# First x tile of a gated S5/GELU kernel: its first slab by a DMA transpose on SyncE, its second by a plain load on ScalarE's queue

## The chip, the core and the metric

The kernel runs on one core of one Trainium2 chip. The metric is the device time of one execution in microseconds (us), taken as the median of several runs. Beside it there is one profiled execution, whose trace and profile page are read below.

## What is computed

x is 2048 tokens by 640 channels in bf16. Two branches read it and a gate for each token mixes them:

```python
g = sigmoid((x * gate_w).sum(-1, keepdims=True))
# branch a: a diagonal state-space model (S5)
Lam_bar = exp(exp(log_dt) * Lam);  B_bar = ((Lam_bar - 1) / Lam)[:, None] * B      # complex
Bu = x @ B_bar.T
h[t] = Lam_bar * h[t-1] + Bu[t]                                                  # over 2048 steps
a = 2 * real(h @ C.T) + x * Dskip
# branch b: a dense layer with GELU, F = 1728
b = gelu(x @ w1 + b1) @ w2 + b2
out = g * a + (1 - g) * b
```

## The kernel before

The tokens are worked on in four tiles (q = 0 to 3) of 512. TensorE needs x with channels on partitions, so each tile has a transposed copy `xT[q]`, which has five slabs of 128 channels x 512 tokens (k = 0 to 4). A second copy with tokens on partitions, `xn`, feeds the gate on VectorE. The weights `w1`, `B`, `w2` and `C` are loaded once and stay in SBUF.

TensorE's order is: a warm-up on constants (`warm`, L416), the first part of the GELU layer for tile 0 (`m1_first`, L653), the rest of that layer for tile 0 (`m1`, L675), the projection with B (`bproj`, L718), and then, tile by tile, the second dense layer (L1015, L809), the projection with C (L1085, L922), B and `m1` again. VectorE builds tables from Lambda and runs the scan. ScalarE evicts PSUM and applies GELU.

Every piece of work is an `op(...)` with an engine, an assumed duration, an assumed latency `lat`, the names that it reads and writes, and a priority. `Sched.order` (L43) simulates the engines with those assumed times and puts the operations of each engine in an order; this order is fixed when the kernel is built. So an engine waits at run time for whatever its next instruction needs, even where a later instruction could run. SyncE (SP) and ScalarE (ACT) also issue DMAs, each on its own queue; an issue takes its place in the order of its engine.

What the start of the kernel looks like:

- SP issues two loads of x (`xna0`, `xna1`: 256 tokens each, the first 256 channels, 128 KB each), then the w1 slabs 1 and 2, a DMA transpose for slab 2 of `xT[0]`, w1 slab 3, a DMA transpose for slabs 3 and 4, w1 slab 4, the rest of w1, and then DMA transposes of B and of the other x tiles.
- ACT issues w1 slab 0 after GpSimd's clearing of `rows` (L386), and then six small loads of vectors into `rows`.
- Slabs 0 and 1 of `xT[0]` are made on TensorE: eight 128x128 transposes through PSUM (`xt0` to `xt3`, L428, each two transposes) and four VectorE copies (`xc0` to `xc3`, L434). The first half of the tokens goes first, a filler matmul (`fill`, L441) stands behind it, and the first six output blocks of slab 0 are computed in halves of 256 tokens.
- `m1_first` computes eight output blocks of 128 features in eight PSUM banks, one slab at a time: for each slab k the blocks jf = 0 to 7. Two of these matmuls, (k 0, jf 7) and (k 1, jf 7), are put back behind slab 2's first seven, because bank 7 is used by the transposes and by `cols`.
- `cols` (L455) is one TensorE transpose of `rows`. VectorE copies its result (L460), and from there a chain of small ScalarE and VectorE steps, with two loads of ScalarE's tables, leads to the first GELU eviction (L662). `m1`'s first matmul (L675) writes bank 0, which that eviction frees.

Of the kernel before, what the change touches and what calls it, by code (L numbers as in the profile page):

```python
# [9 lines left out]
BF16 = mybir.dt.bfloat16  # L10
# [174 lines left out]
def bass_gated_mix__ssm_conv_s5__dense_activation_gelu__prompt_kernel(  # L185
# [40 lines left out]
    with ExitStack() as es:  # L226
# [83 lines left out]
        def inc(eng, ins):  # L310
            return E.inc(eng, ins, eng + "_s")

        def dma_inc(eng, ins, sem):
            SEM(sem)
            E.count.setdefault(sem, 0)
            ins.then_inc(sems[sem], 16)
            E.count[sem] += 16
            return (sem, E.count[sem])
# [7 lines left out]
        def d_mm(n):  # L326
            return n / 2400.0 + 0.004
# [7 lines left out]

        def load_T(name, sem, pairs, writes, prio, dur, lat=3.0, reads=()):
            def fn():
                t = None
                for dst, src in pairs:
                    t = dma_inc("sp", nc.sync.dma_start_transpose(dst, src), sem)  # L340
                return t
            return op(name, "sp", dur, reads, writes, fn, prio=prio, lat=lat)

# [8 lines left out]

        def xtrans(q, ks, prio, dur):
            load_T(f"xT{q}_{ks[0]}", f"l_xT{q}_{ks[0]}", [(xT[q][:, ks[0]:ks[-1] + 1, :], x2[q * 512:(q + 1) * 512, ks[0] * 128:(ks[-1] + 1) * 128])],
                   [("xT", q, k) for k in ks], prio, dur)

# [9 lines left out]

        KN = 2

        for h in range(2):
            load(f"xna{h}", "sp", f"l_xna{h}", xn[0][:, 2 * h:2 * h + 2, 0:KN * 128],  # L370
                 x2[h * 256:(h + 1) * 256, 0:KN * 128].rearrange("(c p) d -> p c d", p=128), [("xna", h)], 0.2 * h, dur=0.45, lat=2.0 + 0.4 * h)
        w1load(1, "sp", 1)
# [15 lines left out]
        op("rz", "pool", 0.2, (), list(ROWS) + [("b1b", 0), ("b1b", 1), "rz"], f_rz, prio=-90)  # L388
        w1load(0, "act", -110, reads=["rz"])
        for i, (nm, (r0, src)) in enumerate(ROWS.items()):  # L390
# [22 lines left out]
        def f_warm():  # L413
            t = None
            for n in (512,) * 5 + (384,):
                t = nc.tensor.matmul(PS[4][:, 0:n], one.broadcast_to([128, 128]), one.broadcast_to([128, n]), start=True, stop=True)  # L416
            return inc("pe", t)

        op("warm", "pe", 2.7, (), [("bank", 4)], f_warm, prio=-1000)

        for i, (k, c0, c1) in enumerate(((0, 0, 2), (1, 0, 2), (0, 2, 4), (1, 2, 4))):
            bank = (7, 6, 7, 6)[i]
            pt = PS[bank][:, :].bitcast(BF16)[:, 0:(c1 - c0) * 128]

            def f_xt(k=k, pt=pt, c0=c0, c1=c1):
                t = None
                for c in range(c0, c1):
                    t = nc.tensor.transpose(pt[:, (c - c0) * 128:(c - c0 + 1) * 128], xn[0][:, c, k * 128:(k + 1) * 128], ident[:, :])  # L428
                return inc("pe", t)

            op(f"xt{i}", "pe", 0.11 * (c1 - c0), [("xna", c0 // 2), "ident"], [("bank", bank)], f_xt, prio=-990 + i if i < 2 else 3.1 + 0.1 * i)

            def f_xc(k=k, pt=pt, c0=c0, c1=c1):
                return inc("dve", nc.vector.tensor_copy(out=xT[0][:, k, c0 * 128:c1 * 128], in_=pt))  # L434

            op(f"xc{i}", "dve", 0.42, [("bank", bank)], [("xT", 0, k, c0)], f_xc, prio=-2000 + i)

        def f_fill():
            t = None
            for _ in range(1):  # L440
                t = nc.tensor.matmul(PS[3][:, 0:256], one.broadcast_to([128, 128]), one.broadcast_to([128, 256]), start=True, stop=True)  # L441
            return inc("pe", t)

        op("fill", "pe", 0.11, [("xna", 0), "ident"], [("bank", 3)], f_fill, prio=-900)

        XK0 = [[("xT", 0, k)] for k in range(KD)]
        XK0[0] = [("xT", 0, 0, 0), ("xT", 0, 0, 2)]
        XK0[1] = [("xT", 0, 1, 0), ("xT", 0, 1, 2)]
        XT = {q: [("xT", q, k) for k in range(KD)] for q in range(1, NQ)}
        XT[0] = [t for x in XK0 for t in x]  # L450

# [4 lines left out]

        op("cols", "pe", 0.3, list(ROWS) + [("b1b", 0), ("b1b", 1), "ident"], [("bank", 7)], f_cols, prio=20.5)

# [130 lines left out]
        for ci, src in enumerate((A_B_re, A_B_im)):  # L589
            for i, (p0, p1) in enumerate(((0, 512), (512, KP * 128))):  # L590
                load_T(f"B{ci}{i}", f"l_B{ci}{i}", [(BT[:, ci, :, p0:p1], src[p0:p1, :])], [("BT", ci, i)], prio=30 + ci + 0.1 * i, dur=0.8 * (p1 - p0) / 128)
        xtrans(1, range(KD), 32, 3.4)
        load("gwb", "sp", "l_gwb", gwb[:, :], gate_w.partition_broadcast(128), ["gwb"], prio=32.2)
        load("xnb", "sp", "l_xnb", xn[0][:, :, KN * 128:D], x2[0:512, KN * 128:D].rearrange("(c p) d -> p c d", p=128),
             [("xn", 0, 0), ("xn", 0, 1)], 32.4, dur=1.0, lat=6.0, reads=[("xna", 0), ("xna", 1)])
        big = load("w2a", "sp", "l_w2a", W2sb[:, 0:NF - 1, :], B_w2[0:nmain, :].rearrange("(j p) d -> p j d", p=128), ["w2a"], prio=33, lat=8.0)
# [46 lines left out]
        def m1_first():  # L643
            late = [(0, NW - 1), (1, NW - 1)]
            seq = [(k, jf) for k in range(KD) for jf in range(NW) if (k, jf) not in late]
            i = seq.index((2, NW - 1))
            seq[i:i] = late
            steps = [(0, jf, h) for h in range(2) for jf in range(6)] + [(k, jf, None) for k, jf in seq if k or jf > 5]
            for k, jf, h in steps:
                t0, t1 = (0, 512) if h is None else (256 * h, 256 * h + 256)  # L650

                def f_mm(jf=jf, k=k, t0=t0, t1=t1):
                    return inc("pe", nc.tensor.matmul(PS[jf][:, t0:t1], W1sb[:, k, jf * 128:(jf + 1) * 128], xT[0][:, k, t0:t1],  # L653
                                                      start=(k == 0 and t0 == 0), stop=(k == KD - 1), skip_group_check=jf < 6))

                op(f"m1_0_{jf}_{k}_{t0}", "pe", d_mm(t1 - t0), (XK0[k] if h is None else XK0[k][h:h + 1]) + [w1tok(k, jf)], [("bank", jf)],
                   f_mm, prio=pe_prio())
            for jf in range(NW):
                ctr["bank"] += 1

                def f_ge(jf=jf):
                    return inc("act", nc.scalar.activation(Gl[0][:, jf, :], PS[jf][:, :], ACT.Gelu_apprx_tanh, bias=b1col[:, jf:jf + 1]))  # L662

                op(f"ge_0_{jf}", "act", d_act(512), [("bank", jf), "b1col"], [("gl", 0, jf)], f_ge, prio=10)
# [344 lines left out]
        def outsT(q, mid=None):  # L1009
# [58 lines left out]
            for d in range(KD):  # L1068

                def f_dx(d=d):  # L1070
                    for _ in range(14 if q == NQ - 2 else 0):
                        nc.scalar.nop(nofuse=True)
                    return inc("act", nc.scalar.activation(xT[q][:, d, :], xT[q][:, d, :], ACT.Copy, scale=cols2[:, 1, d:d + 1]))  # L1073

                op(f"dx_{q}_{d}", "act", d_act(512), [("cols2", 1)], XK0[d] if q == 0 else [("xT", q, d)], f_dx, prio=20)

# [125 lines left out]
```

## Time and profile before

| | |
|---|---|
| device time, median of 3 runs | 212.66 us (212.58 to 212.69) |
| device time of the profiled execution | 211.84 us |
| span of its trace, first to last instruction | 210.5 us |
| TensorE matmul busy | 206.9 us (98%) |
| VectorE / ScalarE busy | 191.0 us (91%) / 102.7 us (49%) |
| mean granted clock in the record | 1.000 |

The trace's span starts with the first instruction and ends with the last; 1.34 us of the profiled execution's own time lie around it. The profiled execution is 0.82 us shorter than the median of the runs, so differences are worked out within the trace and put on the median. A line such as `4.55 0.39 PE L428 MATMUL ... x4` of the timeline reads: start, time from the first start to the last end, engine, line of the kernel, operation, tiles, and how many instructions are merged. PE is TensorE's matmul side, PEld its weight loads; SPq and ACTq are the DMA issues of SyncE and ScalarE. A matmul's record is longer than the distance to the next one, because they are pipelined.

### The profile page before, as it was taken

The numbers are of one execution on the slowest core, as the hardware profiler recorded it, in microseconds if no ns is written. First come the engines' busy times: TensorE is split into PE (matmuls) and PEld (weight loads), VectorE is DVE, ScalarE is ACT, GpSimd is POOL, SyncE is SP. The second block draws the span as 40 slices with busy tenths as digits, with TensorE's granted clock in tenths as the row PEclk, the third lists the DMA queues.
The fourth block names the chain that finished last, engine by engine and source line by source line (L and its number), as shares of the span: only waits on it lengthen the run. The fifth ranks groups of instructions, "written<-read, shape, count | busy, mean of one in ns | idle before, by whom it ended". The sixth has DMA issues, their size and how long they took to land.

```text
span 210.5 us, 2557 instructions
## 1 busy us (share of the span) xinstructions
PE 206.9 (98%) x987; PEld 95.1 (45%) x1004; DVE 191.0 (91%) x244; ACT 102.7 (49%) x166; POOL 4.2 (2%) x12
## 2 busy tenths in 40 slices
PE   8999999999999999999999999999999999999996
PEld 4544444444444444444444444444444444444444
DVE  2499999999999999999999999899999999899482
ACT  2398556679850533556683222455664253204321
POOL 1000000030000000000000000000010000000000
DMA  6999999999500020053373000006631000006623
GB/s 191 271 230 124 200 204 226 361 190 207 129 0 4 0 50 0 0 107 65 80 61 113 3 0 0 0 2 140 142 87 58 0 0 4 0 2 145 135 71 100
DMA packets 50248, 19.47 MB, mean 93 GB/s; under 512 B 43068, under 2 KB 48828, under 8 KB 50236
## 3 DMA queue, kind: packets, MB, share of 16 engines
q1 hardware_dynamic: 47904, 17.59, 38.2%
q0 software_dynamic: 1600, 1.32, 4.3%
q10 hardware_dynamic: 732, 0.40, 0.7%
q8 instruction: 8, 0.13, 0.3%
q14 instruction: 4, 0.03, 0.1%
HBM read 8.68 MB, written 2.63 MB: 54 GB/s over the span
## 4 chain that ended last, share of the span: by engine, by line
PE 98%; issue 0%; DVE 0%
PE ps L675 22%; PE ps L718 20%; PE ps L1015 20%; PE ps L1085 15%; PE ps L809 5%; PE ps L653 4%; PE ps L922 4%; PE ps L829 1%; PE ps L416 1%; PE ps L696 1%; PE ps L882 1%; PE ps L1050 1%; PE ps L428 0%; PE ps L846 0%; DVE W1sb L954 0%
## 5 line engine op out<-in xcount | busy, mean ns | idle before, releaser
L675 PE MATMUL ps<-xT,W1sb 128*128 128x512 bf16 x214 | 47.5, 379 | 0.3
L762 DVE TENSOR_TENSOR_SCAN W<-atab,V 128x1280 bf16<-128x1280 f32 x16 | 44.3, 2812 | 0.3
L718 PE MATMUL ps<-xT,BT 128*128 128x512 bf16 x196 | 43.3, 379 | 0.2
L1015 PE MATMUL ps<-Gl,W2sb 128*128 128x512 bf16 x192 | 42.8, 379 | 0.2
L682 ACT ACTIVATE Gl<-ps,cols 128x512 bf16<-128x512 f32 x44 | 29.8, 695 | 15.5 <-PE ps L675 15.5
L675 PEld LDWEIGHTS ps<-xT,W1sb 128*128 128x128 bf16 x220 | 21.5, 98 | 26.0
L1085 PE MATMUL ps<-Hb,CT 128*128 128x512 bf16 x150 | 32.9, 379 | 0.0
L729 ACT ACTIVATE U<-ps 128x512 bf16<-128x512 f32 x40 | 23.7, 596 | 15.5 <-PE ps L718 15.5
L718 PEld LDWEIGHTS ps<-xT,BT 128*128 128x128 bf16 x200 | 19.4, 98 | 23.8 <-ACT Gt L704 0.4
L1015 PEld LDWEIGHTS ps<-Gl,W2sb 128*128 128x128 bf16 x195 | 18.9, 98 | 23.3 <-issue 0.7
L1023 ACT ACTIVATE E1T<-ps,cols 128x512 bf16<-128x512 f32 x15 | 10.0, 686 | 26.2 <-PE ps L1015 14.7
L1085 PEld LDWEIGHTS ps<-Hb,CT 128*128 128x128 bf16 x150 | 14.7, 98 | 17.7
L1093 ACT ACTIVATE E2T<-ps 128x512 bf16<-128x512 f32 x15 | 9.0, 597 | 21.7 <-PE ps L1085 21.7
L627 DVE SCALAR_TENSOR_TENSOR trf<-xn,gwb 128x640 bf16<-128x640 bf16 x16 | 13.2, 823 | 0.4
L505 DVE TENSOR_TENSOR V<-V,W 128x1280 bf16<-128x1280 bf16 x16 | 12.5, 821 | 0.3
L505 DVE TENSOR_TENSOR Hb<-Hb,V 128x1280 bf16<-128x1280 bf16 x16 | 12.5, 821 | 0.3
L505 DVE TENSOR_TENSOR V<-mr,U 128x2560 bf16<-128x2560 bf16 x8 | 11.9, 1492 | 0.3
L505 DVE TENSOR_TENSOR Hb<-c,W 128x2560 bf16<-128x2560 bf16 x8 | 11.9, 1490 | 0.2
L809 PE MATMUL ps<-W2sb,Gl 128*128 128x512 bf16 x51 | 11.8, 379 | 0.1
L505 DVE TENSOR_TENSOR V<-s,W 128x2560 bf16<-128x2560 bf16 x8 | 11.9, 1484 | 0.0
L505 DVE TENSOR_TENSOR W<-mi,U 128x2560 bf16<-128x2560 bf16 x8 | 11.9, 1483 | 0.0
L1073 ACT ACTIVATE xT<-xT,cols 128x512 bf16<-128x512 bf16 x15 | 10.0, 712 | 0.0
(103 smaller groups left out, 148.2 us busy)
## 6 DMA issues: line engine op xcount, KB each, us to landing
W2sb<-in_B_w_dram SPq DMA_DIRECT2D x1, 2080.0 KB, 8.4
out_dram<-xn SPq DMA_DIRECT2D x3, 640.0 KB, 5.5
xn<-in_A_x_dram POOLq DMA_DIRECT2D x2, 640.0 KB, 7.0
W1sb<-in_B_w_dram SPq DMA_DIRECT2D x4, 256.0 KB, 4.0
trf<-grow SPq DMA_DIRECT2D x4, 256.0 KB, 4.9
xn<-in_A_x_dram SPq DMA_DIRECT2D x1, 640.0 KB, 7.2
W1sb<-in_B_w_dram SPq DMA_DIRECT2D x1, 480.0 KB, 5.6
W1sb<-in_B_w_dram SPq DMA_DIRECT2D x1, 400.0 KB, 6.4
```

The lines of the kernel that those rows point to most:

```text
L505: return inc("dve", nc.vector.tensor_tensor(out=o, in0=a, in1=b, op=o_))
L627: t = inc("dve", nc.vector.scalar_tensor_tensor(out=scr[:, :], in0=xn[q % 2][:, c, :], scalar=1.0, in1=gwb[:, :], op0=ALU.mult, op1=ALU.mu ...
L675: t = nc.tensor.matmul(PS[bank][:, :], W1sb[:, k, jf * 128:(jf + 1) * 128], xT[q][:, k, :], start=(k == 0), stop=(k == KD - 1))
L682: return inc("act", nc.scalar.activation(Gl[q % 2][:, jf, :], PS[bank][:, :], ACT.Gelu_apprx_tanh, bias=b1col[:, jf:jf + 1]))
L718: t = nc.tensor.matmul(PS[bank][:, :], BT[:, ci, kd, k * 128:(k + 1) * 128], xT[q][:, kd, :], start=(kd == 0), stop=(kd == KD - 1))
L729: return inc("act", nc.scalar.activation(dst, src, ACT.Copy, scale=1.0 if ci == 0 else -1.0))
L762: t = inc("dve", nc.vector.tensor_tensor_scan(out=g[:, ci, :], data0=a, data1=v[:, ci, :], initial=0.0, op0=ALU.mult, op1=ALU.add))
L809: t = nc.tensor.matmul(PS[bank][:, :], Gl[q % 2][:, jf, t4 * 128:(t4 + 1) * 128], W2sb[:, jf, 0:DN], start=False, stop=False, skip_group_c ...
L1015: t = nc.tensor.matmul(PS[bank][:, :], W2sb[:, jf, d * 128:(d + 1) * 128], Gl[q % 2][:, jf, :], start=(jf == 0 and not lead), stop=(jf == ...
L1023: return inc("act", nc.scalar.activation(E1T[:, d, :], PS[bank][:, :], ACT.Identity, bias=cols2[:, 0, d:d + 1]))
L1073: return inc("act", nc.scalar.activation(xT[q][:, d, :], xT[q][:, d, :], ACT.Copy, scale=cols2[:, 1, d:d + 1]))
L1085: t = nc.tensor.matmul(PS[bank][:, :].rearrange("p (s t) -> p s t", s=2), CT[:, ci, k, d * 128:(d + 1) * 128], Hb[:, 2 * (q % 2):2 * (q % ...
```

## The change

Slab 0 of `xT[0]` is loaded by one DMA transpose of 512 tokens x 128 channels, which is SP's first instruction. Slab 1 is loaded with tokens on partitions, by one plain load of 512 rows of 256 bytes (128 KB), which ACT issues behind w1 slab 0; four TensorE transposes and one VectorE copy of 512 columns make it. The w1 slab 0 load no longer waits for the clearing of `rows`. The warm-up gets one more matmul of 512 columns, the filler goes, slab 0's matmuls are whole (512 tokens), and `cols` comes earlier in `m1_first`. The later load of the rest of `xn` becomes two loads, since channels 0 to 127 have not been loaded in that layout.

```diff
-        for h in range(2):
-            load(f"xna{h}", "sp", f"l_xna{h}", xn[0][:, 2 * h:2 * h + 2, 0:KN * 128],
-                 x2[h * 256:(h + 1) * 256, 0:KN * 128].rearrange("(c p) d -> p c d", p=128), [("xna", h)], 0.2 * h, dur=0.45, lat=2.0 + 0.4 * h)
+        xtrans(0, range(0, 1), 0, 1.2)
         w1load(1, "sp", 1)
...
-        w1load(0, "act", -110, reads=["rz"])
+        w1load(0, "act", -110)
+        load("xna", "act", "l_xna", xn[0][:, :, 128:256], x2[0:512, 128:256].rearrange("(c p) d -> p c d", p=128), ["xna"], -109, dur=0.5, lat=2.4)
...
-            for n in (512,) * 5 + (384,):
+            for n in (512,) * 6 + (384,):
...
-        for i, (k, c0, c1) in enumerate(((0, 0, 2), (1, 0, 2), (0, 2, 4), (1, 2, 4))):
...
+        def f_xt():
             t = None
+            for c in range(4):
+                t = nc.tensor.transpose(ptx[:, c * 128:(c + 1) * 128], xn[0][:, c, 128:256], ident[:, :])
             return inc("pe", t)
+        op("xt", "pe", 0.44, ["xna", "ident"], [("bank", 7)], f_xt, prio=5.5)
+        def f_xc():
+            return inc("dve", nc.vector.tensor_copy(out=xT[0][:, 1, :], in_=ptx))
+        op("xc", "dve", 0.6, [("bank", 7)], [("xT", 0, 1)], f_xc, prio=-2000)
...
-        op("cols", "pe", 0.3, list(ROWS) + [("b1b", 0), ("b1b", 1), "ident"], [("bank", 7)], f_cols, prio=20.5)
+        op("cols", "pe", 0.3, list(ROWS) + [("b1b", 0), ("b1b", 1), "ident"], [("bank", 7)], f_cols, prio=17.5)
...
-        load("xnb", "sp", "l_xnb", xn[0][:, :, KN * 128:D], x2[0:512, KN * 128:D].rearrange("(c p) d -> p c d", p=128),
-             [("xn", 0, 0), ("xn", 0, 1)], 32.4, dur=1.0, lat=6.0, reads=[("xna", 0), ("xna", 1)])
+        for i, (f0, f1) in enumerate(((0, 128), (256, D))):
+            load(f"xnb{i}", "sp", f"l_xnb{i}", xn[0][:, :, f0:f1], x2[0:512, f0:f1].rearrange("(c p) d -> p c d", p=128),
+                 [("xn", 0, 0), ("xn", 0, 1)][i:i + 1], 32.4 + 0.1 * i, dur=1.0, lat=6.0, reads=["xna"])
...
         def m1_first():
-            steps = [(0, jf, h) for h in range(2) for jf in range(6)] + [(k, jf, None) for k, jf in seq if k or jf > 5]
...
+            for k, jf in seq:
+                def f_mm(jf=jf, k=k):
+                    return inc("pe", nc.tensor.matmul(PS[jf][:, :], W1sb[:, k, jf * 128:(jf + 1) * 128], xT[0][:, k, :],
+                                                      start=(k == 0), stop=(k == KD - 1)))
+                op(f"m1_0_{jf}_{k}", "pe", d_mm(512), [("xT", 0, k), w1tok(k, jf)], [("bank", jf)], f_mm, prio=pe_prio())
```

In the order that results, TensorE runs: seven warm-up matmuls, the four transposes of `xt`, seventeen matmuls of `m1_first`, `cols`, and the other twenty-three matmuls of `m1_first`. Behind that its order is the same in both kernels. SP runs: the DMA transpose of slab 0, w1 slabs 1 and 2, and the rest as before.

## The prediction

> **What bounds the kernel now.** I read the page's busy shares and chain first, then the timeline of the first 14 us, then the DMA issues with their times to landing, then single stretches.
>
> The page's first and fourth parts:
>
> ```profile
> PE 206.9 (98%) x987; PEld 95.1 (45%) x1004; DVE 191.0 (91%) x244; ACT 102.7 (49%) x166; POOL 4.2 (2%) x12
> ...
> PE 98%; issue 0%; DVE 0%
> ```
>
> TensorE is the chain from beginning to end, and in the list of waits no other engine and no DMA holds it for more than 0.6 us: twice for a slab copy of VectorE (0.6 together) and once for the first x load (0.5), all before 5.3 us. So whatever moves the moment at which TensorE gets through `m1_first` moves the end by the same amount. The reference point is L675's first matmul, the end of `m1_first`. The timeline of the start, some lines left out:
>
> ```profile
> 0.74 0.97 SPq L333 DMA_DIRECT2D xn<-in_A_x_dram  x2
> 0.78 2.61 PE L416 MATMUL ps<-const-bfloat16-1.0 128*128 128x512 bf16 x6 [0.78 <-PEq L1187]
> 0.97 0.40 ACTq L333 DMA_DIRECT2D W1sb<-in_B_w_dram  x1
> 2.74 1.20 SPq L340 DMA_TRANSPOSE xT<-in_A_x_dram  x1
> 3.06 0.49 PEld L428 LDWEIGHTS ps<-ident,xn 128*128 128x128 bf16 x4 [0.47 <-DMA xn<-in_A_x_dram]
> 3.19 0.63 PE L428 MATMUL ps<-ident,xn 128*128 128x128 bf16 x4
> 3.61 0.42 PE L441 MATMUL ps<-const-bfloat16-1.0 128*128 128x256 bf16 x1
> 3.99 0.72 PE L653 MATMUL ps<-xT,W1sb 128*128 128x256 bf16 x3
> 4.55 0.39 PE L428 MATMUL ps<-ident,xn 128*128 128x128 bf16 x4
> 4.77 2.99 PE L653 MATMUL ps<-xT,W1sb 128*128 128x256 bf16 x17
> 7.60 0.22 PE L455 MATMUL ps<-ident,rows 128*128 128x128 bf16 x1
> 12.06 4.73 ACT L662 ACTIVATE Gl<-ps,cols 128x512 bf16<-128x512 f32 x8
> 13.27 5.56 PE L675 MATMUL ps<-xT,W1sb 128*128 128x512 bf16 x25
> ```
>
> Useful matmuls start at 3.99, because the x halves come one after the other: the second half is transposed (4.55) while the first half's products run. L675 starts at 13.27. From the DMA issues:
>
> ```profile
> xn<-in_A_x_dram SPq DMA_DIRECT2D x2, 128.0 KB, 2.6
> W1sb<-in_B_w_dram ACTq DMA_DIRECT2D x1, 256.0 KB, 2.8
> out_dram<-Gl ACTq DMA_DIRECT2D x1, 128.0 KB, 1.9
> Gl<-xT SPq DMA_TRANSPOSE x1, 2.4
> ```
>
> Asked one by one, the x halves, issued at 0.74 and 1.27, take 2.3 and 2.9 us and so land at 3.04 and 4.17.
>
> **The change, step by step.** Call L the landing of the new slab 1 load and M the start of `m1_first`. In the new order the four transposes of `xt` stand ahead of all of `m1_first`, though slab 0's matmuls do not need them. So TensorE cannot use slab 0 when it lands; M is set by the last of slab 0, w1 slab 0 and `xt`, and `xt` waits for a load that is second on ScalarE's queue.
>
> *Slab 0's DMA transpose.* No row has it on an empty queue from HBM. Low: the last transpose of the kernel, same 128x512 size from SBUF, 2.4 us from issue to landing, so 0.74 + 2.4 = 3.14. High: slab 2's, 4.2 us behind two w1 slabs, so 4.94. I take 3.6, nearer the first, because nothing is ahead of it in its queue.
>
> *w1 slab 0.* It no longer waits for the memset that ended at 0.94, starts at 0.74 instead of 0.97, and with its 2.8 us lands at 3.54.
>
> *Slab 1's load.* Its issue starts at 0.74 + 0.40 + 0.03 = 1.17 (0.03 is the gap from 1.37 to the next issue on that queue at 1.40). Before, the same 512 KB (two x halves and w1 slab 0) first moved at 1.80 and had landed by 4.17. Now the bytes start later: the last transpose's bytes began 1.2 us after its issue (205.45 against 204.26), so here at 1.94. That gives 4.17 + 0.14 = 4.31. Besides, w1 slab 1, which stood behind both x halves in one queue, now has only 128 KB ahead of it on SyncE's and can run beside slab 1's load. If all of its 256 KB went first, that would be 0.8 us (the stretch 3.4 to 4.4 moves 319 GB/s), L = 5.1. But from 2.5 to 3.5 ScalarE's queue moved 0.24 MB and SyncE's 0.10 MB, so ScalarE's is not the one that is starved; I add 0.14, and L = 4.45. Low end: w1 slab 0's 3.54 plus 128 KB at that rate, 3.9. High end: 1.17 + 4.2 = 5.4. [...]
>
> *From L to M.* From the first half's landing (3.04) to its first transpose (3.19) is 0.15. Four transposes took 0.42 at the slow pace (3.19 to 3.61) and 0.22 at the full one (4.55 to 4.77). They would start at 4.60, just after the pace doubled (between 4.39 and 4.55), so I take the middle, 0.32: M = 4.45 + 0.47 = 4.92.
>
> *From M to L675.* Forty matmuls of 512 columns at 0.216 (25 of them lie between 13.43 and 18.83 in the chain, 5.40) are 8.64, and `cols` 0.06: 8.70. This leaves out what before paid inside `m1_first`: four transposes (0.22), the slow first products and the wait for the second half.
>
> *`cols` earlier, a new wait.* Before, 5.15 us lie between `cols` (7.60) and the end of the first GELU (12.06 + 0.69), which frees bank 0. Now only 23 matmuls stand between `cols` and L675: 0.06 + 4.97 = 5.03. The chain behind `cols` is the same, so L675 waits 0.12 and the hand-over, say 0.15, behind which all of TensorE is queued. With 0.69 against 1.08 us per bank, later banks do not wait.
>
> *At nothing:* the memset wait and the extra warm-up matmul (0.43, done by 3.6 while TensorE would wait for slab 1 anyway; if slab 1 came at 3.1 it would cost up to 0.4). VectorE's one copy of 512 columns for four of 0.29: slab 1's products are due 7 x 0.216 = 1.5 after M. SyncE's queue: one issue of 1.20 for two that took 0.97, so all that follows is 0.24 later. w1 slab 1 (issued 1.75, took 3.8) then lands near 5.8 and is due at 6.4; slab 2 (2.74 + 4.2) near 7.2, due at 7.9. Behind those, the split load adds one issue of 0.5 and 128 KB near 24 us, for a gate step at 49 us. VectorE's table chain is later by M + 17 x 0.216 - 7.60 = 1.0; the first H that TensorE needs (71.8) was done at 67.9, and VectorE idles 0.75 at 182.9, so this is covered; the cover is 3.9 us.
>
> *Sum.* L675 starts at 4.92 + 8.70 + 0.15 = 13.77 against 13.27: +0.50 us. Everything behind it keeps order and pace. The profiled execution would take 211.84 + 0.50 = 212.34, and the median 212.66 + 0.50 = 213.16. In general the difference is L - 3.95. About 0.2% (0.43 us) is what a measurement of this kernel can tell from no change; it lies at L = 4.38.
>
> **Rivals.**
>
> *The clock goes late (slower).* Before, TensorE was fed almost without a gap from 0.78, and its pace doubled 3.7 us later, at about 4.5. Now it stands still from 3.6 to 4.6. If that gap decides, and the 3.7 us count anew from 4.6, the half pace lasts until 8.3, and the matmuls from 5.0 on lose half of 3.3: +1.65, with the transposes at the slow pace +0.1, on top of 0.50: 214.9. For it: a gap of 1.0 where before had 0.2 or less. Against: the added warm-up matmul, and most of the stretch is still busy. The granted clock is no help, its column reads 1.00 even from 0.70 to 3.40. [...]
>
> *ScalarE's queue is served first (faster).* If w1 slab 0 and slab 1's load go ahead of everything, slab 1 lands at 1.17 + 1.9 = 3.07 by the kernel's last store, and M is 3.64 (0.15 + 0.42 later; w1 slab 0 is there by 3.54). Until 4.5 the products run at the slow pace, which loses 0.43: L675 at 3.64 + 8.70 + 0.43 + 0.15 = 12.92, -0.35, 212.3. With the pace already doubled, thanks to the longer warm-up, it is -0.78, 211.9. Against: the 256 KB ahead of it in its own queue.
>
> *No use of slab 0, and no loss either (no change).* L near 3.95 gives 212.66: what is saved (transposes and halves inside `m1_first`) pays for the later start. It is the low side of the forecast's own range.
>
> **How the numbers follow.** The forecast, `xt`'s load sets the start: 0.72, of which 0.24 with L below 4.38 (within 0.2%) and 0.48 above. Late clock: 0.11, slower. ScalarE's queue first: 0.15, 0.09 of it faster by over 0.2% and 0.06 within. Something else that leaves the time as it is: 0.02. Sums: faster 0.09, same 0.32, slower 0.59. The range takes the forecast's ends (L = 3.9: -0.05; L = 5.4: +1.45, rounded up for the slow transposes) and the first price of the faster rival (-0.35): 212.3 to 214.2. Outside are the late clock and the faster rival's second price, 0.20.
>
> **What would show it.** Right: the weight load of `xt` waits for the x load from 3.6 or so to about 4.5, with slab 0 landed before; products start near 4.9; L675 near 13.8 with a short wait on ScalarE's first GELU; no other wait on TensorE. Wrong: `xt` starts before 4.0; matmuls of 512 columns 0.43 apart after 5; or a wait at w1 slab 1 or slab 2, which would mean that the transpose holds up SyncE's queue by more than 0.24.

## The result

| | before | changed |
|---|---|---|
| device time, median (lowest to highest, runs) | 212.62 us (212.20 to 212.69, 4) | 214.62 us (214.54 to 214.99, 4) |
| ratio to before, 95% interval | | 1.0102 (1.0084 to 1.0119) |
| profiled execution / span of its trace | 211.84 / 210.5 us | 214.64 / 213.3 us |
| start of `m1`'s first matmul | 13.27 (L675) | 16.09 (L655) |

The changed kernel is 2.0 us slower in the medians and 2.80 us slower in the two profiled executions. All of the latter lies ahead of `m1`: its first matmul comes 2.82 later, and what follows it keeps its order and its length. The forecast was 213.16 with a range up to 214.2, so the sign was right and the size was not.

The busy shares and the chain on the profile page of the changed kernel:

```profile
PE 209.6 (98%) x994; PEld 94.7 (44%) x994; DVE 190.4 (89%) x241; ACT 102.7 (48%) x166; POOL 4.2 (2%) x12
...
PE 97%; DMA 2%; ACTq 0%; DVE 0%; issue 0%
```

TensorE is still the chain, but 2% of it, the first 3.56 us behind ACT's issue, is now a DMA. TensorE is also busy 2.7 us longer (209.6 against 206.9), though the change takes 256 columns of its work away (512 more of warm-up, 256 of filler and 512 of transposes less), and this is the first sign that something other than a wait was lost. (The counts x994 and x987 do not compare, since a trace lacks some matmul records: the traces of these kernels have 977 to 1004.) The timeline of the start (lines are those of the changed kernel: L413 is the warm-up, L423 `xt`, L634 `m1_first`, L438 `cols`, L655 `m1`):

```profile
0.74 0.40 ACTq L333 DMA_DIRECT2D W1sb<-in_B_w_dram  x1
0.74 1.23 SPq L340 DMA_TRANSPOSE xT<-in_A_x_dram  x1
0.78 3.04 PE L413 MATMUL ps<-const-bfloat16-1.0 128*128 128x512 bf16 x7 [0.78 <-PEq L1167]
1.17 0.45 ACTq L333 DMA_DIRECT2D xn<-in_A_x_dram  x1
...
4.78 0.61 PE L423 MATMUL ps<-ident,xn 128*128 128x128 bf16 x4 [0.96 <-DMA xn<-in_A_x_dram]
5.18 5.78 PE L634 MATMUL ps<-xT,W1sb 128*128 128x512 bf16 x17
10.79 0.22 PE L438 MATMUL ps<-ident,rows 128*128 128x128 bf16 x1
...
15.26 4.74 ACT L642 ACTIVATE Gl<-ps,cols 128x512 bf16<-128x512 f32 x8
16.09 5.55 PE L655 MATMUL ps<-xT,W1sb 128*128 128x512 bf16 x25
```

The warm-up is done by 3.8, TensorE waits 0.96 for slab 1, the transposes start at 4.78 and the products at M = 5.18. The seventeen matmuls then take 5.6 us up to `cols`, where the full pace (0.216 each) would take 3.7. The same stretch cut at 9.0 has nine of them:

```profile
5.18 4.04 PE L634 MATMUL ps<-xT,W1sb 128*128 128x512 bf16 x9
```

With 0.63 for the last record (each of the nine lasts 631 ns), nine matmuls in 4.04 are (4.04 - 0.63) / 8 = 0.426 apart. TensorE works at half its pace until about 9.1; from there on the matmuls stand 0.216 apart as before. Ten steps of 0.426 instead of 0.216 explain about 1.95 us (the step that spans the doubling is shorter). The windows of the same trace (busy us and count by engine, then the granted clock, DMA share, GB/s) show that the clock column says nothing of it; it reads 1.00 in every stretch:

```profile
core 0: us, PE busy (x) PEld busy (x) DVE busy (x) ACT busy (x) POOL busy (x), PEclk, DMA share, GB/s
0.78:3.80 3.02, 3.02 (x7) 0.84 (x7) 0.49 (x3) 0.00 (x0) 0.58 (x4) 1.00 0.72 166
3.80:4.78 0.98, 0.02 (x2) 0.01 (x1) 0.00 (x0) 0.28 (x1) 0.00 (x0) 1.00 0.99 140
4.78:9.10 4.32, 4.32 (x14) 1.80 (x15) 0.42 (x1) 1.00 (x1) 0.00 (x0) 1.00 1.13 257
9.10:16.00 6.90, 6.88 (x33) 2.95 (x31) 4.42 (x15) 4.30 (x8) 0.00 (x0) 1.00 1.16 258
```

What landed when, from the DMA issues of the start (last column: us from issue to landing):

```profile
W1sb<-in_B_w_dram ACTq DMA_DIRECT2D x1, 256.0 KB, 2.8
...
xn<-in_A_x_dram ACTq DMA_DIRECT2D x1, 128.0 KB, 3.6
xT<-in_A_x_dram SPq DMA_TRANSPOSE x1, 4.2
```

So w1 slab 0 was there at 3.54 and slab 1 at 4.73; the transpose of slab 0, issued at 0.74, landed at 4.93, after slab 1. The list of waits has two new entries that matter:

```profile
PE ps L423 <- DMA xn<-in_A_x_dram: 1.0, 1, 1.0
...
PEld ps L655 <- issue: 0.6, 1, 0.6
```

The first is the standstill. The second is the weight load of `m1`'s first matmul, which is held back until the first GELU, done at 15.26 + 0.69 = 15.95, has freed its bank: the last matmul of `m1_first` starts at 15.60, the next would follow at 15.81, and it starts at 16.09.

### The profile page after: what moved, and what is told of

It is laid out like the page before. It is cut to its first block, busy times and chain, and to the rows that moved or that the text cites. A ratio compares the mean times of both kernels' runs of the same rounds, so it can differ in the third digit from the quotient of the medians.

```text
span 213.3 us, 2553 instructions
## 1 busy us (share of the span) xinstructions
PE 209.6 (98%) x994; PEld 94.7 (44%) x994; DVE 190.4 (89%) x241; ACT 102.7 (48%) x166; POOL 4.2 (2%) x12
## 4 chain that ended last, share of the span: by engine, by line
PE 97%; DMA 2%; ACTq 0%; DVE 0%; issue 0%
PE ps L655 22%; PE ps L698 20%; PE ps L995 20%; PE ps L1065 15%; PE ps L789 5%; PE ps L634 5%; PE ps L902 4%; DMA xn<-in_A_x_dram 2%; PE ps L809 1%; PE ps L676 1%; PE ps L862 1%; PE ps L1030 1%; PE ps L423 0%; PE ps L826 0%; ACTq L333 0%; DVE W1sb L934 0%
## 5 line engine op out<-in xcount | busy, mean ns | idle before, releaser
L655 PE MATMUL ps<-xT,W1sb 128*128 128x512 bf16 x220 | 48.1, 379 | 0.1
L698 PE MATMUL ps<-xT,BT 128*128 128x512 bf16 x200 | 43.8, 379 | 0.0
L655 PEld LDWEIGHTS ps<-xT,W1sb 128*128 128x128 bf16 x220 | 21.4, 98 | 26.3 <-issue 0.6
L634 PE MATMUL ps<-xT,W1sb 128*128 128x512 bf16 x40 | 10.8, 437 | 0.0
```

The lines of the kernel that those rows point to most:

```text
L634: return inc("pe", nc.tensor.matmul(PS[jf][:, :], W1sb[:, k, jf * 128:(jf + 1) * 128], xT[0][:, k, :], start=(k == 0), stop=(k == KD - 1)))
L655: t = nc.tensor.matmul(PS[bank][:, :], W1sb[:, k, jf * 128:(jf + 1) * 128], xT[q][:, k, :], start=(k == 0), stop=(k == KD - 1))
L698: t = nc.tensor.matmul(PS[bank][:, :], BT[:, ci, kd, k * 128:(k + 1) * 128], xT[q][:, kd, :], start=(kd == 0), stop=(kd == KD - 1))
```

## The experiments

The theory after this trace: the 1 us in which TensorE stands still before slab 1 keeps it at half pace for longer. The rival: the load alone is the cost, and the pace doubles at a moment of its own. Ratios are to runs of the kernel before on the same chip, with 95% intervals. In each short diff `-` is the kernel named and `+` the experiment.

**The kernel before, unchanged**, gives the spread of one kernel.

> The kernel before, unchanged, for a second trace. Its first profiled execution took 211.84 us against a median of 212.62, 0.78 less than its other runs. Theory (the pace of TensorE doubles late when TensorE stands still before it): before has no standstill over 0.5 us, so the pace doubles at 4.4 to 4.6 us from the span's start again, and L675's first matmul starts within 0.3 us of 13.27. Rival (the moment of the doubling is chance, a window that runs on its own, and the changed kernel only had bad luck): the moment lies elsewhere, by up to some 3 us, and the time goes with it.

212.24 us (211.87 to 212.71, 10 runs), ratio 0.9994 (0.9979 to 1.0009). The 28 runs beside it go from 211.70 to 213.14, an even spread of 1.4 us. In this trace the pace doubled at about 4.9 and L675 started at 13.47, 0.20 later than in the first trace, where it was about 4.5. Part of the spread of one kernel is thus the moment of the doubling.

**The changed kernel with a warm-up that covers the wait.**

```diff
-            for n in (512,) * 6 + (384,):
+            for n in (512,) * 9 + (384,):
```

> The changed kernel with ten instead of seven warm-up matmuls, so that TensorE works until 4.7 to 4.9 us, when slab 1's load (landed at 4.73) lets the transposes start. Theory of the standstill: the pace doubles at about 4.5, the matmuls from 5.2 on are 0.216 apart, the 1.95 us lost at the slow pace come back: 212.6 to 212.9, ratio to before 1.000 to 1.002. Rival (data: the time is lost because slab 0 and slab 1 land late): no gain, 214.6. Rival (chance): no gain on average beyond a few tenths.

212.93 us (212.56 to 213.48, 10 runs), ratio 1.0034 (1.0018 to 1.0050). The timeline of its start:

```profile
0.78 3.59 PE L413 MATMUL ps<-const-bfloat16-1.0 128*128 128x512 bf16 x10 [0.78 <-PEq L1167]
4.61 0.40 PE L423 MATMUL ps<-ident,xn 128*128 128x128 bf16 x4 [0.24 <-DMA xn<-in_A_x_dram]
4.85 4.04 PE L634 MATMUL ps<-xT,W1sb 128*128 128x512 bf16 x17
```

The loads are where they were (slab 1 at 4.57, M = 4.85), but the pace has doubled at 3.49, within the warm-up, and `cols` comes 3.9 us after M instead of 5.6. Filler alone brings back 214.62 - 212.93 = 1.7 of the 2.0 us, and none of the ten runs is near 214.5. The standstill is the main cost, and the rival falls.

**The kernel before with a standstill**, made by a shorter warm-up:

```diff
-            for n in (512,) * 5 + (384,):
+            for n in (512,) * 2:
```

> The kernel before with two warm-up matmuls instead of six, so that TensorE stands still from 1.6 to 3.06 us, while no data comes later and nothing waits for the warm-up. Theory of the standstill: the pace doubles some 4.4 us after work resumes at 3.06, at 7.5 or so instead of 4.5; the matmuls from 4.5 to 7.5 lose half: +1.5 us, 214.1. Rival (data): no change, 212.6. Rival (chance): no change on average.

212.80 us (212.40 to 213.94, 10 runs), ratio 1.0028 (1.0010 to 1.0047), a third of what had been expected.

```profile
0.78 1.01 PE L416 MATMUL ps<-const-bfloat16-1.0 128*128 128x512 bf16 x2 [0.78 <-PEq L1187]
3.21 0.61 PE L428 MATMUL ps<-ident,xn 128*128 128x128 bf16 x4 [1.42 <-DMA xn<-in_A_x_dram]
```

Here TensorE stands still for 1.42, longer than in the changed kernel, and yet the pace doubled at about 6.7, only 3.5 after work began again at 3.21. The standstill ends 1.6 earlier than the changed kernel's 4.78, which fits the smaller cost. So its length alone does not decide; the section on the prediction works out what its place does.

**The transposes behind four of slab 0's matmuls** (the assumed latency and a priority of the changed kernel), so that TensorE starts as soon as slab 0 is there:

```diff
-  load("xna", "act", ..., ["xna"], -109, dur=0.5, lat=2.4)
+  load("xna", "act", ..., ["xna"], -109, dur=0.5, lat=3.6)
-  op("xt", "pe", 0.44, ..., f_xt, prio=5.5)
+  op("xt", "pe", 0.44, ..., f_xt, prio=4.5)
```

> The changed kernel with the four transposes of slab 1 behind the first four matmuls of slab 0 instead of ahead of all. It tells what the place of the transposes costs, the step of the prediction that set the start. Slab 0's transposed load landed at 4.94, later than slab 1's at 4.73, so slab 0's matmuls can start at about 5.0 instead of 5.18; TensorE stands still 0.2 us longer. If the place were the cause of the loss: -1 us or more. Theory of the standstill: -0.2 to +0.3 us against the changed kernel, 214.4 to 214.9, the slow pace stays until 9 us or later.

214.47 us, ratio 1.0077 (1.0037 to 1.0117), in two groups: 212.78, 212.83 and 212.87, and four runs from 214.47 to 215.33. The profiled execution is the 215.33:

```profile
4.92 1.89 PE L634 MATMUL ps<-xT,W1sb 128*128 128x512 bf16 x4 [1.10 <-DMA xT<-in_A_x_dram]
6.60 0.63 PE L423 MATMUL ps<-ident,xn 128*128 128x128 bf16 x4
```

Slab 0 lands no earlier than slab 1 (4.87 and 4.67). The first product starts at 4.92 instead of 5.18, but the transposes now stand behind it, and the pace doubled only at 10.19. That one program has two groups, 1.6 us apart with nothing between them, asks for the changed kernel's own groups.

**The changed kernel again.**

> The changed kernel again, for the spread of its times and a second trace. So far: its first runs lay at 214.5 to 215.0 (pace doubled at 9.11); with the transposes moved, single runs lay at 212.8 to 212.9 or at 214.5 to 215.3, nothing between (the traced one doubled at 10.19); the kernel before doubled at about 4.5 and 4.9 in two traces, with a gap in its warm-up at 6.7. Theory now (standstill and chance together): TensorE's pace doubles at the end of a window of some 3.4 us that starts at a random moment, and only if TensorE worked in more than some three quarters of it. Kernel before: any window end after 3.4 us does, so times spread evenly over some 1.5 us. Changed kernel: a window that holds the whole standstill from 3.8 to 4.8 fails, so the runs fall in two groups, about one in three near 213.0 and two in three from 214.3 to 215.4. Rival (a doubling that always comes some 4.4 us after the standstill): one group near 214.6. Rival (chance without the standstill): one even spread like that of before.

Six runs: 212.78, 213.18, 214.56, 214.69, 215.12 and 215.17; ratio 1.0133 (1.0112 to 1.0154). With the first four, two runs of ten are in the early group and eight in the late one. The profiled execution is the 212.78, so the forecast's own case can be read as well. Its start, and `m1`'s first matmuls with the GELU before them:

```profile
0.78 3.04 PE L413 MATMUL ps<-const-bfloat16-1.0 128*128 128x512 bf16 x7 [0.78 <-PEq L1167]
4.72 0.40 PE L423 MATMUL ps<-ident,xn 128*128 128x128 bf16 x4 [0.91 <-DMA xn<-in_A_x_dram]
4.96 4.15 PE L634 MATMUL ps<-xT,W1sb 128*128 128x512 bf16 x17
8.94 0.22 PE L438 MATMUL ps<-ident,rows 128*128 128x128 bf16 x1
...
13.40 1.84 ACT L642 ACTIVATE Gl<-ps,cols 128x512 bf16<-128x512 f32 x3
14.23 0.59 PE L655 MATMUL ps<-xT,W1sb 128*128 128x512 bf16 x2
```

The same warm-up, the same standstill (0.91) and nearly the same landings, but the four transposes and all that follows run at the full pace, which came at about 4.20, inside the standstill. Only the moment of the doubling differs.

**One more warm-up matmul** (`(512,) * 6` to `(512,) * 7`), which halves the standstill.

> The changed kernel with eight instead of seven warm-up matmuls: TensorE works until about 4.2 us and stands still for some 0.5 us instead of 0.9 to 1.0. Theory (a window of some 3.4 us from a random start, which must be busy for about three quarters; the traces so far put the bound between 72% that failed and 79% that passed): a window with all of this standstill in it is still 85% busy, so no window fails, the late group at 214.5 to 215.2 is gone, and all runs lie between 212.6 and 213.8 with a median near 213.0. Rival (any standstill while the first products are awaited starts the count anew): a group from 214.4 up remains.

212.86 us (212.56 to 213.47, 12 runs), ratio 1.0027 (1.0003 to 1.0050).

```profile
4.72 0.40 PE L423 MATMUL ps<-ident,xn 128*128 128x128 bf16 x4 [0.48 <-DMA xn<-in_A_x_dram]
```

The wait before `xt` is 0.48, and all twelve runs are in the early group. In these runs the size of the standstill decides: 0.48 put none of twelve runs into the late group, 0.91 to 0.96 put eight of ten there.

**What is left beside the clock.** Two more edits were put on top of the long warm-up, each alone and then both: `cols` sooner (`prio=17.5` to `prio=14.5`), and slab 1's load ahead of w1 slab 0 on ACT's queue (`-109` to `-111`).

> The changed kernel with ten warm-up matmuls, and cols three matmuls sooner, with 26 matmuls of m1_first behind it as in the kernel before instead of 23. Theory (L675's first matmul waits for the first GELU because cols comes too late): the wait of 0.28 us seen in the changed kernel goes, 212.93 becomes 212.6 to 212.75, ratio to before 1.001 to 1.003. Rival (the wait is another, a weight slab or the bank): no change, 212.9.

212.66 us (212.15 to 213.26, 12 runs), ratio 1.0024 (1.0009 to 1.0038), against 1.0034 (1.0018 to 1.0050) without; the intervals overlap. The trace says it more clearly: no line of L655 is left in the list of waits, and `m1` starts at 13.94 where it was 14.02.

> The changed kernel with ten warm-up matmuls, and slab 1's load ahead of w1 slab 0 on ScalarE's queue. Theory (slab 1's landing is set by the 256 KB ahead of it in its own queue): it lands at 3.2 to 3.6 instead of 4.57 to 4.73, w1 slab 0 at 3.8 to 4.2; the start is then set by slab 0's transposed load, which does not move (4.8 to 4.9), so the time stays within 0.2 us of 212.93. Rival (all loads share the DMA engines evenly, and position does not matter): slab 1 lands at 4.4 or later.

212.85 us (212.29 to 213.47, 10 runs), ratio 1.0030 (1.0015 to 1.0045): no gain. Its DMA issues:

```profile
W1sb<-in_B_w_dram ACTq DMA_DIRECT2D x1, 256.0 KB, 3.4
xn<-in_A_x_dram ACTq DMA_DIRECT2D x1, 128.0 KB, 2.5
xT<-in_A_x_dram SPq DMA_TRANSPOSE x1, 4.1
```

Slab 1 now lands at 3.27, but w1 slab 0 goes to 4.66 and slab 0 stays at 4.88, so products could not start much before 4.9 either way. (M is 5.29 in this trace: its pace doubled at about 5.25 only, and the ten warm-up matmuls at half pace keep the transposes back until 4.89.) What slab 1 gains, slab 0 and w1 slab 0 do not give.

> The changed kernel with three things mended at once: ten warm-up matmuls, cols three matmuls sooner, slab 1's load ahead of w1 slab 0 on ScalarE's queue. Theory (what is left against before is the later start, 4.9 to 5.3 instead of 4.0, less the transposes and halves that before has inside m1_first): no wait for w1 slab 1 (it landed at 5.5 with slab 1 first) and none for the first GELU, 212.4 to 212.6, ratio to before 1.0005 to 1.002. If it were below before (rival: the loads in the new form are as good, and only the order around them was bad): 212.1 or less.

212.36 us (212.08 to 213.28, 12 runs), ratio 0.9998 (0.9975 to 1.0022). With all three edits the changed kernel is level with the kernel before (median 212.20 beside it), and not faster; `m1` starts at 14.00 in its trace.

**Why slab 0 is late.** All four loads of the start were put on SP's queue with the transpose first, on top of the long warm-up:

```diff
-        w1load(0, "act", -110)
-        load("xna", "act", ..., -109, dur=0.5, lat=2.4)
+        w1load(0, "sp", 0.5)
+        load("xna", "sp", ..., 0.7, dur=0.5, lat=2.4)
```

> For landings alone: the changed kernel with ten warm-up matmuls, and w1 slab 0 and slab 1's load issued by SyncE behind slab 0's DMA transpose, so that the transpose has the DMA engines to itself. It landed 4.05 to 4.2 us after its issue beside ScalarE's two loads, against the 3.6 (2.9 us) that the prediction took. Theory (it is slowed by ScalarE's loads, which move their bytes first): 2.4 to 3.0 us, landing at 3.2 to 3.8. Rival (a DMA transpose from HBM takes some 4 us by itself): landing at 4.7 to 4.9 again. The time itself is of no use here, since w1 slab 0 comes later.

213.75 us in its single run. The DMA issue of the transpose, with no large load beside it:

```profile
xT<-in_A_x_dram SPq DMA_TRANSPOSE x1, 2.8
```

Issued at 0.74, slab 0 lands at 3.56, near the 3.6 that the prediction took. Beside the loads of ACT's queue the same transpose takes 4.0 to 4.2. But w1 slab 0 and slab 1, now behind it, land at 5.37 and 5.76, and more is lost than won.

**The memset wait.** The prediction had put the removal of this wait "at nothing". Alone, on the kernel before:

```diff
-        w1load(0, "act", -110, reads=["rz"])
+        w1load(0, "act", -110)
```

> One part of the change alone in the kernel before: w1 slab 0's load no longer waits for the clearing of rows, issued at 0.74 instead of 0.97. The prediction put this at nothing for the start. Theory: the first products wait for VectorE's copy of the x half (3.93), not for w1 slab 0 (3.77, then about 3.55), so nothing changes, ratio 0.999 to 1.001; the second x half may land up to 0.2 us earlier or later, since ScalarE's bytes go first. Rival: w1 slab 0 ahead of the first x half delays it and the start, +0.2 us or more.

214.16 us (212.33 to 214.87, 10 runs), ratio 1.0061 (1.0027 to 1.0095). Leaving out that one wait costs 2.0 us in the medians (212.20 beside it) and 1.3 us by the ratio; the ten runs lie spread from 212.33 to 214.87 and not in two groups. The DMA issue of the first half of x and the timeline of its start:

```profile
xn<-in_A_x_dram SPq DMA_DIRECT2D x1, 128.0 KB, 3.3
```

```profile
4.10 0.61 PE L428 MATMUL ps<-ident,xn 128*128 128x128 bf16 x4 [0.71 <-DMA xn<-in_A_x_dram]
4.50 0.42 PE L441 MATMUL ps<-const-bfloat16-1.0 128*128 128x256 bf16 x1
4.88 0.82 PE L653 MATMUL ps<-xT,W1sb 128*128 128x256 bf16 x3
```

With w1 slab 0 issued 0.22 earlier, its bytes move first (by 3.0 us ACT's queue had moved 0.24 MB and SyncE's 0.04 MB, where before it was 0.18 and 0.13 MB), and the first half of x takes 3.3 instead of 2.3 us. The kernel before now has a standstill of 0.71 as well, its pace doubles at 9.99 in this trace, and L675 starts at 16.30. None of the changed kernel's new loads is needed for a loss of this kind, which makes this an independent witness for what a standstill costs.

The reverse, the changed kernel with that wait given back to both loads on ACT's queue:

```diff
-        w1load(0, "act", -110)
+        w1load(0, "act", -110, reads=["rz"])
-        load("xna", "act", ..., lat=2.4)
+        load("xna", "act", ..., lat=2.4, reads=["rz"])
```

> The changed kernel with the memset wait ahead of w1 slab 0 put back (issue at 0.97 instead of 0.74; slab 1's load 0.23 later too). Theory (ScalarE's bytes get ahead of slab 0's because they are asked for 0.23 us earlier): slab 0's transposed load lands at 3.6 to 4.1 instead of 4.9. Slab 1's load, which the start waits for, lands no earlier, 4.6 to 5.0, so the standstill and the two groups of times stay, median near 214.6. Rival (the DMA transpose is slowed by any load beside it, whichever was first): slab 0 lands at 4.7 to 5.0 again.

214.62 us (212.95 to 215.64, 11 runs), ratio 1.0102 (1.0072 to 1.0131): the same as the changed kernel, three runs early and eight late.

```profile
W1sb<-in_B_w_dram ACTq DMA_DIRECT2D x1, 256.0 KB, 3.4
xT<-in_A_x_dram SPq DMA_TRANSPOSE x1, 4.0
xn<-in_A_x_dram ACTq DMA_DIRECT2D x1, 128.0 KB, 3.5
```

The transpose's first bytes now move at 2.09 instead of 2.55, ahead of the others, yet slab 0 lands at 4.73. Beside plain loads the transpose is slow here even where it goes first (4.0 us, against 2.8 alone). Removing the memset wait is not what delays slab 0 here.

**Slab 0's matmuls first, with that wait and `cols` sooner** (the edits of three experiments above, with the changed kernel's own warm-up).

> The same with the four transposes of slab 1 behind the first four matmuls of slab 0 and cols three matmuls sooner. Theory: the start is set by slab 0 and w1 slab 0, at 4.0 to 4.3; the standstill from 3.8 shrinks to 0.5 us or less, so the late group goes; slab 2 still lands near 8.1, 5.7 us before L675, which then starts at 13.8 or later: 212.2 to 212.6, ratio to before 1.000 to 1.002. If slab 0 stays late (rival of the run before): as the changed kernel with its transposes moved, two groups, 212.8 and 214.5 to 215.3. Below 212.0 would mean that the new form of the loads beats the kernel before.

214.09 us (212.69 to 214.98, 9 runs, four early and five late), ratio 1.0078 (1.0050 to 1.0107). Slab 0 landed at 4.78 and the standstill was 1.01, so the order of the transposes could not help.

## Why the prediction was wrong

**The step that failed is "From M to L675": all forty matmuls of `m1_first` at 0.216.** It rests on the words "just after the pace doubled (between 4.39 and 4.55)". That moment was read from one trace of the kernel before and carried over to a kernel whose TensorE stands still for 1 us around it. In the late trace the pace doubled at 9.11. From M to `m1` it took 10.91, where 8.70 + 0.15 had been summed; 1.95 of the difference is the half pace, the other 0.1 a longer wait for the first GELU.

The prediction had this case as a rival, "the clock goes late", and the chance of 0.11 that it gave was the mistake beside it. The rival's place was right and its price near: 214.9 us was worked out, and the eight late runs of the changed kernel lie from 214.54 to 215.17. Its mechanism was right in part. A count that begins anew at 4.6 would have made every run late and ended the half pace at 8.3; but two of ten runs were early, and the late trace doubled at 9.11. That 214.9 falls among the runs is partly luck: in the traces `m1` came 2.82 later, where this rival's sum has 2.25, and the trace from which the sum starts was 0.8 shorter than the median of its runs. The reason given against it, "most of the stretch is still busy", looked at how long TensorE had been fed on the whole, where, by the estimate below, it is how much of one stretch of 3.41 us the standstill takes, and so a case that holds most runs lay outside the range.

Where the doubling falls can be read from the traces. In eight of them the granted clock has a record of its own, behind the column of means: it sets in at the doubling (9.11 in the changed kernel's first trace, 4.20 in its second), and its next entry comes 204.800 or 208.213 us later. The two differ by 3.413 and are 60 and 61 times that. From these numbers comes an estimate of the author's: the pace changes only at the ends of equal windows of 3.413 us, which lie at another phase in each run. How busy TensorE was in such a window was measured. Counting back from the doubling, the windows view gives the busy matmul time, here for the changed kernel's late and early trace:

```profile
2.28:5.70 3.42, 2.46 (x10) 0.94 (x9) 0.28 (x1) 1.20 (x1) 0.00 (x0) 1.00 1.00 245
5.70:9.11 3.41, 3.41 (x10) 1.17 (x9) 0.14 (x1) 0.08 (x1) 0.00 (x0) 1.00 1.19 241
...
0.79:4.20 3.41, 3.03 (x7) 0.83 (x7) 0.49 (x3) 0.00 (x0) 0.57 (x4) 1.00 0.81 168
```

Behind the first the pace stayed at half, behind the other two it had doubled. For all eight, as a share of 3.41:

| trace | doubled at | that window busy | the window before it, busy |
|---|---|---|---|
| warm-up covers the wait | 3.49 | 79% | |
| the same, `cols` sooner | 4.18 | 100% | |
| changed, early group | 4.20 | 89% | |
| slab 0's matmuls first | 4.33 | 85% | |
| memset wait given back | 8.48 | 100% | 66% |
| changed, late group | 9.11 | 100% | 72% |
| before, without memset wait | 9.99 | 100% | 79% |
| transposes behind four matmuls | 10.19 | fed throughout (5.18 of 5.20 us from 4.90) | 68% |

In these eight traces windows of 66 to 72% left the pace at half, behind windows of 85% and more it had doubled, and 79% went both ways (at half pace a record lasts 0.63 and the next matmul starts 0.43 after it, so at the end of the work this measure may be up to 0.2 us, some 6% of a window, too high). In the six traces with a standstill of 0.71 or more in this place, the time of the execution goes with the doubling: 212.78 and 212.69 with a doubling at 4.20 and 4.33, and 214.44, 214.64, 214.85 and 215.33 with one at 8.48, 9.11, 9.99 and 10.19.

From these numbers the chance can be estimated, if every phase of the window is equally likely. If the limit is taken at 79%, a window may be idle for 0.72. In the changed kernel TensorE works from 0.78, stands from 3.82 to 4.78, and works on. A window of 3.41 then passes the first time if it ends between 3.47 (where 0.72 of it lies before 0.78) and 4.54 (0.72 after 3.82); at a random phase that is 1.07 / 3.41 = 31%. Otherwise, by the same estimate, the pace doubles one window later, between 7.95 and 10.29, and the loss is half of what lies between M = 5.18 and there, 1.4 to 2.6 us. The runs: 12 of 37 were early in the four kernels with a standstill of 0.91 to 1.17 (2 of 10 for the changed kernel, 3 of 7 with the transposes behind four matmuls, 3 of 11 with the memset wait given back, 4 of 9 with slab 0's matmuls first), and in the changed kernel late runs lie 1.4 to 2.4 above early ones (214.54 - 213.18 and 215.17 - 212.78). With a standstill of 0.48, less than 0.72, every window should pass, and no run of twelve was late. The kernel before, fed from 0.78 with no gap over 0.5, should always pass at the first or second such end, its doubling moving between about 3.5 and 6.9; half of what lies behind its first products at 4.0 is lost, up to 1.4 us, which is the spread of its runs.

Two things do not fit this estimate. One run of the kernel before, beside the memset experiment, took 214.93, far outside that spread; it has no trace, and its cause is open. And for the kernel before with two warm-up matmuls the same working puts the doubling between 5.90 and 9.31, so that from its trace (6.72, 212.78) the runs should lie between 212.4 and 214.1. They go from 212.40 to 213.94, but seven of ten lie below 212.9, where equally likely phases would put about three.

**The forecast's own sum was also too small, by 0.46.** In the early trace L655 starts at 14.23 where 13.77 was worked out. The terms:

- L, slab 1's landing: 4.67 for 4.45 (+0.22). With all of w1 slab 1 moved first the prediction had worked out 5.1; the measured value lies between the two.
- From L to M: 0.29 for 0.47 (-0.18). The first transpose came 0.05 after the landing instead of 0.15, and the four took 0.24 instead of 0.32, because in this group the pace has doubled before them. M is 4.96 for 4.92. In the late trace the slow transposes take it back: L = 4.73, M = 5.18.
- w1 slab 1: predicted near 5.8 and due at 6.4, it landed at 6.64, and the first matmul of k = 1 started at 6.78 instead of 6.47 (+0.31). This wait was not in the sum. The prediction moved SyncE's later loads by 0.24, the difference of the issues; the bytes came later by more. In the late trace it is hidden, since at half pace slab 1's products are due at 8.17 and the load lands at 6.75.
- The first GELU: 4.96 + 8.70 + 0.31 = 13.97, so the wait is 0.26 for 0.15 (+0.11). The GELU ends at 13.40 + 0.69 = 14.09, as far behind `cols` as before (5.15); the hand-over from ScalarE to TensorE is 0.14, and the prediction had left 0.03 for it.

Together +0.46. Against the traces of before this is +0.96 (13.27) or +0.76 (13.47).

**"At nothing: the memset wait" was wrong by its reason.** The prediction counted 0.23 gained for w1 slab 0 and did not ask which load loses. On the kernel before this edit alone costs 0.6% (0.3 to 1.0). In the changed kernel it costs nothing that shows, since slab 0 and slab 1 are late with it or without (slab 0 lands at 4.73 or 4.93, and `xt`, which waits for slab 1, starts at 4.99 or 4.78).

**Slab 0's transpose came at the high end:** it landed at 4.93 where 3.6 was taken and 4.94 was the bound. "Nothing is ahead of it in its queue" was true, and what slowed it was beside it, in the other queue (2.8 us with nothing large beside it, 4.2 here). In the early trace the weight load of the first product waits for it (0.3), so that M hangs on both loads nearly alike.

**The faster rival** (ScalarE's queue served first, slab 1 at 3.07) did not come: 4.73. Even with slab 1 first in its queue, at 3.27, the products started no sooner.

**Right were** the sign; that everything is decided ahead of `m1` and moves the end one for one; w1 slab 0 at 3.54; the standstill of about 1.0; that `xt`'s load ends the standstill; and that moving `cols` makes a wait for the first GELU. Two of the signs named for being wrong came: matmuls 0.43 apart after 5, and, in the early trace, a wait at w1 slab 1. One wording was off: `cols` was said to come earlier. Counted in matmuls that are left behind it, it comes later (23 instead of 26), and only therefore is there a wait.

**Left open.** Why the transpose slows down beside plain loads is not shown; the runs only bound it (2.8 alone, 4.0 to 4.2 beside them). Its packets tell where the time goes. Alone, its bytes move from 2.10 to 3.05 and it lands at 3.56; in the changed kernel they move from 2.55 to about 3.6 and it lands at 4.93. So some 0.8 of the 1.4 lies behind its last byte, and 0.45 ahead of its first. A transpose that starts alone, with w1 slab 0 and slab 1 held back just so long that both are in time, wasn't tried.

## What to carry to other kernels

At the start of a kernel, keep TensorE fed until its pace has doubled (in the traces here between 3.49 and 10.19 us): a filler matmul that a sum counts at nothing can be worth more than an earlier load, and here one of them, put into 0.43 us of idle time, saves 1.8 us in the medians. Price a standstill near the first few microseconds as a chance and not as a surcharge (here 0.48 us made none of twelve runs late, and 0.91 to 1.17 made 25 of 37 late), and when run times of one kernel fall into two groups, compare the spacing of the first matmuls before looking for anything else. An edit that lets one of the first loads go sooner can take that time from a load beside it (w1 slab 0 from the first half of x, 2.3 to 3.3; slab 1 from w1 slab 0, which then landed at 4.66), so name the one that loses.

## What the runs showed of the hardware

A DMA transpose of 512 x 128 from HBM took 2.8 us alone and 4.0 to 4.2 beside 384 KB of plain loads from the other queue. A plain load of the same 128 KB, first in its queue and with other loads beside it, took 2.3 to 2.5, and 3.3 where w1 slab 0 was issued at the same time.

Little moved for a while behind the transpose's bytes in two traces. The data rate of the one-queue experiment, from 1.5 to 5.5 us in slices of 0.1:

```profile
GB/s 0 0 0 0 13 0 92 151 151 207 246 215 167 75 26 8 0 0 0 118 92 85 61 61 123 248 248 348 369 430 300 306 287 286 274 192 146 225 200 123
```

From 3.1 to 3.4 nothing moves, though the next load had been issued at 2.04 (in the other traces the first bytes of the first plain loads came 1.0 to 1.7 after their issue, so this gap alone says little), and then the rate stays near or below 120 GB/s until 4.0, where the later slices reach 430. In the changed kernel the rate falls to 41 to 123 GB/s from 4.0 to 4.6, again behind the transpose's last byte. In the kernel before, whose queue starts with two plain loads, w1 slab 1 follows them without such a drop: 309 GB/s in the mean from 3.5 to 4.5. So the drop stood behind the transpose in these two traces and was absent in the one without it there; its cause is not shown.

The page's granted clock read 1.00 in all these stretches, at half pace and at full; on it only the spacing of the matmuls (0.426 or 0.216) tells them apart.
